# Attention over long keys: both softmax reductions across partitions on GpSimd's all-reduce, with the other small steps moved to ScalarE and VectorE

## The chip, the cores and the metric

The kernel runs on one NeuronCore of one Trainium2 chip. The metric is the time of one execution on the device, in microseconds (us). Of each kernel there is also one execution taken by the hardware profiler; its span runs from the first instruction to the last. In the profile PE is TensorE (PEld its weight loads), DVE is VectorE, ACT is ScalarE, POOL is GpSimd and SP is SyncE, which here only issues DMAs. L12 means line 12 of the kernel's file.

## What is computed

```python
    B, H, Sq, Skv, Dh = 16, 32, 4, 4096, 128      # q, k, v: bf16 normal numbers times 0.05
...
def reference(q, k, v):
    scale = q.shape[-1] ** -0.5
    scores = jnp.einsum('bhqd,bhkd->bhqk', q, k) * scale
    attn = _softmax(scores, axis=-1)
    return jnp.einsum('bhqk,bhkd->bhqd', attn, v)
```

There are 16 x 32 = 512 heads. Each has only 4 query rows, but 4,096 rows of K and as many of V, 1 MB each. So each head reads 2 MB from HBM for 4 rows of output of 128 numbers, and the whole problem reads 1,074 MB.

## The kernel before

The work is done head by head. K and V of two heads (a pair, 2 MB) come with one DMA each into rings of `NBK` and `NBV` buffers (three each). In a buffer, partition p holds 32 consecutive rows of a head (32 chunks of 128 columns), so a chunk is a 128x128 block whose rows are keys.

One step per head, with the code's names:

- `T(h)` on PE transposes the 32 chunks of K against `ident` into the four PSUM tiles `ktp`, eight chunks to a tile. DVE copies three of the four tiles and ACT the fourth (`evac`) into `kT`.
- `QK(h)` on PE multiplies each chunk of `kT` with the four query columns in `qT`. It uses 48 moving columns per chunk (`NPAD`), of which only the first four are wanted; the others are overwritten by the next chunk. The result is 128 columns of scores (32 chunks x 4 queries) in the tile `szo`, keys on the partitions.
- `stageA(h)` on DVE takes the maximum over the chunks for each partition and query into `m1` (128x4). POOL then takes the maximum over the 128 partitions (`partition_all_reduce` into `Mb`, L182), and multiplies by -scale (`negm`, L187).
- `exps(h)` on ACT makes four exponentials, one per query, of 128x32 scores with the bias `negm`, into `eT` (bf16).
- `AV(h)` on PE first multiplies `eT` with a matrix of ones (`ones_bf`, four matmuls of 32 columns, L338), which sums over partitions and leaves the sums per chunk in `szo`. Then it accumulates the 32 chunks of V times `eT` in another part of `szo` (L343).
- `stageB(h)` on DVE adds up the sums over the chunks (`Z4`, L251), takes the reciprocal (`rZ`) and multiplies the output with it into `stage`. After 32 heads, PE transposes the collected 128x128 block, DVE copies it to `ob`, and POOL writes it out by a DMA (16 times).

No scheduler orders this. Each engine runs its own list in program order and waits on semaphores that count finished steps. PE's list is, for step i: `T(i+1)`, `QK(i)`, `AV(i-2)` (`LAG` is 2). DVE's is: three evacuations of head i+1, `stageA(i)`, `stageB(i-2)`. ACT's is: the evacuation of head i+1, `exps(i)`. POOL's is: the all-reduce of head i, then its scaling. SP issues K of pair 0 (its two heads apart), then q by a DMA transpose straight into `qT`, and then in turn K of pair g+1 and V of pair g. A K load waits until the transposes of the pair that used its buffer are done (`s_T`), a V load until the AV of the pair that used its buffer is done (`s_oready`).

Two ties matter for following the steps. `T(h)` may fill the fourth `ktp` tile only when ACT has evacuated the head before, and ACT's evacuation of head i+2 comes after `exps(i)` in ACT's list. The four `szo` tiles are used in turn, so `QK(h)` waits until `stageB(h-4)` is done (`s_fin`).

Of the kernel before, what the change touches and what calls it, by code (L numbers as in the profile page):

```python
# [12 lines left out]
def bass_standalone__softmax_full_bidir__sampling_kernel(  # L13
# [17 lines left out]
    CQ = NCH * NQ  # L31
    CPB = 1024 // P
    assert NCH % CPB == 0
    NU = NCH // CPB
    NPAD = 48
    ZBN = 32
    assert CQ % ZBN == 0
    assert (NCH - 1) * NQ + NPAD <= 2 * CQ and 2 * CQ + NPAD <= 384
    scale = float(D) ** -0.5

    NBK = 3
    NBV = 3
    RT = 3
    R = 4
# [10 lines left out]
    with ExitStack() as es:  # L55
# [5 lines left out]
        vN = sb("vN", [P, NBV, 2, NCH * D], BF16)  # L61
        kT = sb("kT", [P, RT, NCH * P], BF16)
        qT = sb("qT", [P, NHD * NQ + NPAD], BF16)
        eT = sb("eT", [P, R, CQ + NPAD], BF16)
        m1 = sb("m1", [P, R, NQ], FP32)
        Mb = sb("Mb", [P, R, NQ], FP32)
        negm = sb("negm", [P, R, NQ], FP32)
        Z4 = sb("Z4", [P, R, NQ], FP32)
        rZ = sb("rZ", [P, R, NQ], FP32)
        ones_bf = sb("ones_bf", [P, P], BF16)  # L70
        ident = sb("ident", [P, P], BF16)
# [6 lines left out]
        s_q = sem("s_q")  # L78
        s_k0 = sem("s_k0first")
        s_k = [sem(f"s_k{i}") for i in range(NBK)]  # L80
        s_v = [sem(f"s_v{i}") for i in range(NBV)]
# [21 lines left out]

        def zb_slot(r):
            return szo[r][:, CQ:2 * CQ]

        def oT_slot(r):
            return szo[r][:, 2 * CQ:2 * CQ + NQ]

        def oT_acc(r):  # L110
            return szo[r][:, 2 * CQ:2 * CQ + NPAD]

# [15 lines left out]
        @block.sync  # L128
        def _(sp):
            def dma_k(g):  # L130
                slot = g % NBK
                if g == 0:
                    for j, sm in ((0, s_k0), (1, s_k[0])):
                        sp.dma_start(  # L134
                            kN[:, 0, j, :],
                            k_h[j].rearrange("(p c) d -> p (c d)", p=P),
                        ).then_inc(sm, 16)
                    return
                if g >= NBK:
                    sp.wait_ge(s_T, NU * (2 * (g - NBK) + 1) + NU)  # L140
                sp.dma_start(
                    kN[:, slot, :, :],
                    k_h[2 * g:2 * g + 2].rearrange("h (p c) d -> p h (c d)", p=P),
                ).then_inc(s_k[slot], 16)

            def dma_v(g):
                slot = g % NBV
                if g >= NBV:
                    sp.wait_ge(s_oready, 2 * (g - NBV) + 2)
                sp.dma_start(  # L150
                    vN[:, slot, :, :],
                    v_h[2 * g:2 * g + 2].rearrange("h (p c) d -> p h (c d)", p=P),
                ).then_inc(s_v[slot], 16)

            dma_k(0)
            sp.dma_start(qT[:, 0:NHD * NQ], q_rows, transpose=True).then_inc(s_q, 16)
            for g in range(NPAIR):
                if g + 1 < NPAIR:
                    dma_k(g + 1)
                dma_v(g)  # L160

        @block.gpsimd
        def _(pool):
# [12 lines left out]

            for hd in range(NHD):
                r = hd % R
                pool.wait_ge(s_m1, hd + 1)
                if hd >= R:  # L180
                    pool.wait_ge(s_e, hd - R + 1)
                pool.partition_all_reduce(  # L182
                    Mb[:, r, :], m1[:, r, :], P, bass.bass_isa.ReduceOp.max
                ).then_inc(s_pl, 1)
                plc += 1
                pool.wait_ge(s_pl, plc)
                pool.tensor_scalar(negm[:, r, :], Mb[:, r, :], -scale, None, op0=ALU.mult).then_inc(s_negm, 1)  # L187
                if done_grp < NGRP and hd == GH * (done_grp + 1) + 10:
                    dma_out(done_grp)
                    done_grp += 1  # L190
# [6 lines left out]
        def _(act):  # L197
# [4 lines left out]
            def exps(hd):  # L202
                r = hd % R
                act.wait_ge(s_negm, hd + 1)
                if hd >= R:
                    act.wait_ge(s_oready, hd - R + 1)
                e_view = eT[:, r, 0:CQ].rearrange("p (c q) -> p q c", q=NQ)
                s_view = sT_slot(hd % NSZ).rearrange("p (c q) -> p q c", q=NQ)
                ins = None
                for qq in range(NQ):  # L210
                    ins = act.activation(  # L211
                        e_view[:, qq, :], s_view[:, qq, :], ACTF.Exp,
                        bias=negm[:, r, qq:qq + 1], scale=scale,
                    )
                ins.then_inc(s_e, 1)
# [10 lines left out]
        def _(dve):  # L226
            dve.memset(ones_bf[:, :], 1.0).then_inc(s_setd, 1)
            dve.memset(qT[:, NHD * NQ:NHD * NQ + NPAD], 0.0).then_inc(s_setd, 1)
# [7 lines left out]
            def stageA(hd):  # L236
# [6 lines left out]
                ).then_inc(s_m1, 1)  # L243

            def stageB(h2):
                r = h2 % R
                z = h2 % NSZ
                gi = h2 // GH
                col = (h2 % GH) * NQ
                dve.wait_ge(s_oready, h2 + 1)  # L250
                dve.tensor_reduce(  # L251
                    Z4[:, r, :], zb_slot(z).rearrange("p (c q) -> p q c", q=NQ), AX.X, ALU.add
                ).then_inc(s_dv, 1)
                dvc[0] += 1
                dve.wait_ge(s_dv, dvc[0])
                dve.reciprocal(rZ[:, r, :], Z4[:, r, :]).then_inc(s_dv, 1)  # L256
                dvc[0] += 1
                dve.wait_ge(s_dv, dvc[0])
                dve.tensor_tensor(  # L259
                    stage[:, gi, col:col + NQ], oT_slot(z), rZ[:, r, :], ALU.mult  # L260
# [4 lines left out]
            def copy_out(gi):  # L265
                dve.wait_ge(s_tp, gi + 1)
                dve.tensor_copy(ob[:, gi, :], tp_slot((tp_step(gi) + 1) % NSZ)).then_inc(s_ob, 1)  # L267

            for u in DVE_UNITS:
                evac(0, u)  # L270
            for i in range(NHD + LAG):
# [3 lines left out]
                if i < NHD:  # L275
                    stageA(i)
                h2 = i - LAG
                if h2 >= 0:
# [5 lines left out]
        def _(pe):  # L284
            pe.wait_ge(s_q, 16)
            pe.wait_ge(s_setd, 3)
            pe.wait_ge(s_setp, 1)
            pending_ob = []

            def T(h):  # L290
# [3 lines left out]
                for u in range(NU):  # L294
                    if u == 0:
                        if h == 0:
                            pe.wait_ge(s_k0, 16)
                        else:
                            pe.wait_ge(s_k[slot], 16 * (g // NBK + 1))
# [30 lines left out]
            def AV(h2):  # L330
# [4 lines left out]
                pe.wait_ge(s_e, h2 + 1)  # L335
                pe.wait_ge(s_v[slot], 16 * (g // NBV + 1))
                for zc in range(CQ // ZBN):
                    pe.matmul(zb_slot(z)[:, zc * ZBN:(zc + 1) * ZBN], lhsT=ones_bf[:, :],  # L338
                              rhs=eT[:, r, zc * ZBN:(zc + 1) * ZBN], start=True, stop=True)
                vview = vN[:, slot, j, :].rearrange("p (c d) -> p c d", d=D)  # L340
# [56 lines left out]
```

## Time and profile before

| what | value |
|---|---|
| time, median of 4 runs | 8304.77 us (8300.1 to 8309.34) |
| profiled execution, its own time | 8303.16 us |
| its span | 8301.4 us |
| PE, DVE, ACT, POOL busy | 2775.2, 1443.1, 885.1, 343.0 us |
| bytes moved by DMA | 1082.20 MB, mean 130 GB/s |
| granted TensorE clock, mean | 0.637 of full speed |

The profile is to be read like this. A row of a group names the line, the engine, the operation and the tiles (result<-operands), then the count, the busy time of all in us, the mean time of one in ns, and the idle time of the engine just before them with what ended it. A line of the waits names the instruction that waited and the one that released it, then the total in us, the number of times and the longest. "issue" as a releaser means that the profile shows nothing that the engine waited for. In the timeline the columns are start and duration in us, and in square brackets the idle time before. PEclk is the clock that the chip granted TensorE, as a share of full speed. In a table of stretches the columns are the stretch, its length, the busy time of PE, PEld, DVE, ACT and POOL with the number of instructions, PEclk, the busy share of the 16 DMA engines, and GB/s. What POOL's records say of custom instructions such as the all-reduce is rough.

### The profile page before, as it was taken

How to read it: one execution, taken by the hardware profiler on the slowest of the kernel's cores; microseconds unless marked ns; L12 is line 12 of the kernel's file. 1: busy time of each engine (PE TensorE's matmuls, PEld its weight loads, DVE VectorE, ACT ScalarE, POOL GpSimd, SP SyncE). 2: the span in 40 equal slices, each digit the busy share in tenths (PEclk: the TensorE clock that was granted, in tenths of full speed). 3: DMA queues.
4: the chain of work that ended last, by engine and by line, in shares of the span. 5: the costliest groups of instructions: out<-in, count | busy, mean ns of one | idle time of the engine just before them, and what ended most of it. 6: DMA issues, size and time to landing. Idle time of an engine off the chain costs nothing.

```text
span 8301.4 us, 115323 instructions
## 1 busy us (share of the span) xinstructions
PE 2775.2 (33%) x51216; PEld 2687.1 (32%) x51216; DVE 1443.1 (17%) x3603; ACT 885.1 (11%) x2561; POOL 343.0 (4%) x1046
## 2 busy tenths in 40 slices
PE   3333333333333333333333333333333333333332
PEld 3333333333333333333333333333333333333332
DVE  1111111111111111111111111111111111111111
ACT  1111111110111111111111111101111111111111
POOL 0000000000000000000000000000000000000000
PEclk6666666666666666666666666666666666666666
DMA  4333333333333333333333333333333333333331
GB/s 185 123 131 132 132 133 127 128 132 132 133 130 128 129 132 132 131 128 128 132 132 132 132 125 131 132 132 132 124 131 132 132 132 128 128 131 132 132 132 72
DMA packets 142366, 1082.20 MB, mean 130 GB/s; under 512 B 10544, under 2 KB 10544, under 8 KB 10800
## 3 DMA queue, kind: packets, MB, share of 16 engines
q1 hardware_dynamic: 141360, 1074.30, 35.0%
q8 instruction: 406, 6.65, 0.3%
q14 instruction: 88, 0.72, 0.0%
q0 software_dynamic: 512, 0.53, 0.0%
HBM read 1073.74 MB, written 0.52 MB: 129 GB/s over the span
## 4 chain that ended last, share of the span: by engine, by line
issue 69%; PE 14%; ACT 10%; POOL 4%; DVE 2%; POOLq 0%; DMA 0%; SPq 0%; ACTq 0%
PE szo L324 8%; PE ktp L308 6%; ACT kT L200 5%; ACT eT L211 4%; POOL Mb L182 2%; DVE m L241 2%; POOL negm L187 2%; POOLq L187 0%; DMA qT<-in_q_dram 0%; PE szo L343 0%; SPq L134 0%; POOL out_dram L175 0%; PE szo L338 0%; DVE Z L251 0%; PE szo L355 0%
## 5 line engine op out<-in xcount | busy, mean ns | idle before, releaser
L308 PE MATMUL ktp<-ident,kN 128*128 128x128 bf16 x16384 | 1518.5, 266 | 5489.1 <-ACT kT L200 5478.9
L308 PEld LDWEIGHTS ktp<-ident,kN 128*128 128x128 bf16 x16384 | 1312.2, 123 | 5576.5 <-ACT kT L200 5566.3
L211 ACT ACTIVATE eT<-szo,negm 128x32 bf16<-128x32 f32 x2048 | 444.3, 333 | 7396.1 <-POOL negm L187 7396.1
L241 DVE TENSOR_REDUCE m<-szo 128x4 f32<-128x128 f32 x512 | 149.4, 292 | 6182.1 <-PE szo L324 6182.1
L234 DVE COPY kT<-ktp 128x1024 bf16<-128x1024 bf16 x1536 | 985.9, 684 | 76.7 <-PE ktp L308 66.6
L324 PE MATMUL szo<-qT,kT 128*128 128x48 bf16 x16384 | 760.1, 216 | 10.0 <-issue 10.0
L324 PEld LDWEIGHTS szo<-qT,kT 128*128 128x128 bf16 x16384 | 744.5, 120 | 10.1 <-issue 10.1
L343 PE MATMUL szo<-eT,vN 128*128 128x48 bf16 x16384 | 714.7, 211 | 0.0
L343 PEld LDWEIGHTS szo<-eT,vN 128*128 128x128 bf16 x16384 | 661.8, 115 | 0.0
L200 ACT COPY kT<-ktp 128x1024 bf16<-128x1024 bf16 x512 | 527.1, 1029 | 12.6 <-PE ktp L308 12.6
L187 POOL TENSOR_SCALAR negm<-Mb 128x4 f32<-128x4 f32 x512 | 131.9, 258 | 4839.1 <-issue 4839.1
L182 POOL PARTITION_ALL_REDUCE Mb<-m x512 | 198.4, 388 | 3110.2 <-issue 3095.1
L251 DVE TENSOR_REDUCE Z<-szo 128x4 f32<-128x128 f32 x512 | 149.3, 292 | 559.2 <-PE szo L343 559.2
L338 PE MATMUL szo<-eT,ones_bf 128*128 128x32 bf16 x2048 | 144.3, 191 | 22.0 <-ACT eT L211 22.0
L338 PEld LDWEIGHTS szo<-eT,ones_bf 128*128 128x128 bf16 x2048 | 108.1, 111 | 22.2 <-ACT eT L211 22.2
L256 DVE RECIPROCAL rZ<-Z 128x4 f32<-128x4 f32 x512 | 91.3, 178 | 17.4
L259 DVE TENSOR_TENSOR stage<-szo,rZ 128x4 bf16<-128x4 f32 x512 | 82.6, 161 | 17.7
L175 POOL DMA_DIRECT2D out_dram<-ob x16 | 12.0, 750 | 5.1 <-DVE ob L267 4.2
L355 PE MATMUL szo<-ident,stage 128*128 128x128 bf16 x16 | 4.1, 253 | 0.8 <-DVE stage L259 0.8
L267 DVE COPY ob<-szo 128x128 bf16<-128x128 bf16 x16 | 3.4, 214 | 0.4 <-PE szo L355 0.4
L355 PEld LDWEIGHTS szo<-ident,stage 128*128 128x128 bf16 x16 | 1.7, 107 | 0.9 <-DVE stage L259 0.9
L200 ACT ACT_TABLE_LOAD x1 | 1.3, 1283 | 0.7 <-PEq L382 0.7
(9 smaller groups left out, 1.3 us busy)
## 6 DMA issues: line engine op xcount, KB each, us to landing
vN<-in_v_dram SPq DMA_DIRECT2D x256, 2048.0 KB, 7.5
kN<-in_k_dram SPq DMA_DIRECT2D x255, 2048.0 KB, 8.6
kN<-in_k_dram SPq DMA_DIRECT2D x2, 1024.0 KB, 6.0
out_dram<-ob POOLq DMA_DIRECT2D x16, 32.0 KB, 1.9
qT<-in_q_dram SPq DMA_TRANSPOSE x1, 8.5
```

Of the source, the lines that this page charges most:

```text
L182: pool.partition_all_reduce(Mb[:, r, :], m1[:, r, :], P, bass.bass_isa.ReduceOp.max).then_inc(s_pl, 1)
L187: pool.tensor_scalar(negm[:, r, :], Mb[:, r, :], -scale, None, op0=ALU.mult).then_inc(s_negm, 1)
L200: act.copy(kT[:, h % RT, u * CPB * P:(u + 1) * CPB * P], ktp[u][:, :]).then_inc(s_eva, 1)
L211: ins = act.activation(e_view[:, qq, :], s_view[:, qq, :], ACTF.Exp, bias=negm[:, r, qq:qq + 1], scale=scale,)
L234: dve.tensor_copy(kT[:, h % RT, u * CPB * P:(u + 1) * CPB * P], ktp[u][:, :]).then_inc(s_evd, 1)
L241: dve.tensor_reduce(m1[:, r, :], sT_slot(hd % NSZ).rearrange("p (c q) -> p q c", q=NQ), AX.X, ALU.max).then_inc(s_m1, 1)
L251: dve.tensor_reduce(Z4[:, r, :], zb_slot(z).rearrange("p (c q) -> p q c", q=NQ), AX.X, ALU.add).then_inc(s_dv, 1)
L256: dve.reciprocal(rZ[:, r, :], Z4[:, r, :]).then_inc(s_dv, 1)
L308: ins = pe.transpose(ktp[u][:, cc * P:(cc + 1) * P], kview[:, c, :], ident[:, :])
L324: ins = pe.matmul(szo[z][:, c * NQ:c * NQ + NPAD], lhsT=ktv[:, c, :], rhs=qT[:, hd * NQ:hd * NQ + NPAD], start=True, stop=True,)
L338: pe.matmul(zb_slot(z)[:, zc * ZBN:(zc + 1) * ZBN], lhsT=ones_bf[:, :], rhs=eT[:, r, zc * ZBN:(zc + 1) * ZBN], start=True, stop=True)
L343: ins = pe.matmul(oT_acc(z), lhsT=vview[:, c, :], rhs=eT[:, r, c * NQ:c * NQ + NPAD], start=(c == 0), stop=(c == NCH - 1),)
```

## The change

- POOL no longer scales the maximum. It now does two all-reduces per head: the maximum of head i, and then the sum of head i-1 (`sum_ar`). Both are `partition_all_reduce`.
- The scaling to `negm` moves to ACT, ahead of the exponentials of the same head.
- The sum of a head's exponentials over the chunks moves to DVE (`rowsum`, on `eT`), which makes `rsum` (128x4) for POOL's sum. The matmuls with ones, the tile `ones_bf` and DVE's reduction over their result are gone. `szo` is laid out anew.
- `stageB` takes the reciprocal of POOL's sum, and waits for the output of AV only ahead of the product.
- q comes by a plain DMA into `qN`; PE transposes it in 16 blocks and DVE copies the blocks to `qT` with 16 copies.
- K has four buffers instead of three, and K of pair g+2 (no longer g+1) is issued after V of pair g. The last pair of K and V comes as two DMAs each, one per head, with a semaphore of its own for the first.

```diff
...
     NGRP = NHD // GH
     CQ = NCH * NQ
     CPB = 1024 // P
     assert NCH % CPB == 0
     NU = NCH // CPB
     NPAD = 48
-    ZBN = 32
-    assert CQ % ZBN == 0
-    assert (NCH - 1) * NQ + NPAD <= 2 * CQ and 2 * CQ + NPAD <= 384
+    OTC = 192
+    assert (NCH - 1) * NQ + NPAD <= OTC and OTC + NPAD <= 384
+    NQC = (NHD * NQ) // P
+    assert (NHD * NQ) % P == 0 and NQC <= 2 * CPB_
     scale = float(D) ** -0.5
 
-    NBK = 3
+    NBK = 4
     NBV = 3
     RT = 3
     R = 4
...
         kN = sb("kN", [P, NBK, 2, NCH * D], BF16)
         vN = sb("vN", [P, NBV, 2, NCH * D], BF16)
         kT = sb("kT", [P, RT, NCH * P], BF16)
+        qN = sb("qN", [P, NQC * D], BF16)
         qT = sb("qT", [P, NHD * NQ + NPAD], BF16)
         eT = sb("eT", [P, R, CQ + NPAD], BF16)
...
+        rsum = sb("rsum", [P, R, NQ], FP32)
...
-        ones_bf = sb("ones_bf", [P, P], BF16)
...
         def sT_slot(r):
             return szo[r][:, 0:CQ]
 
-        def zb_slot(r):
-            return szo[r][:, CQ:2 * CQ]
-
         def oT_slot(r):
-            return szo[r][:, 2 * CQ:2 * CQ + NQ]
+            return szo[r][:, OTC:OTC + NQ]
 
         def oT_acc(r):
-            return szo[r][:, 2 * CQ:2 * CQ + NPAD]
+            return szo[r][:, OTC:OTC + NPAD]
 
         def tp_slot(r):
             return szo[r][:, 384:448].bitcast(BF16)
...
         def _(sp):
             def dma_k(g):
                 slot = g % NBK
-                if g == 0:
-                    for j, sm in ((0, s_k0), (1, s_k[0])):
+                if g >= NBK:
+                    sp.wait_ge(s_T, NU * (2 * (g - NBK) + 1) + NU)
+                if g == 0 or g == NPAIR - 1:
+                    first = s_k0 if g == 0 else s_klast
+                    for j, sm in ((0, first), (1, s_k[slot])):
                         sp.dma_start(
-                            kN[:, 0, j, :],
-                            k_h[j].rearrange("(p c) d -> p (c d)", p=P),
+                            kN[:, slot, j, :],
+                            k_h[2 * g + j].rearrange("(p c) d -> p (c d)", p=P),
                         ).then_inc(sm, 16)
                     return
-                if g >= NBK:
-                    sp.wait_ge(s_T, NU * (2 * (g - NBK) + 1) + NU)
                 sp.dma_start(
                     kN[:, slot, :, :],
                     k_h[2 * g:2 * g + 2].rearrange("h (p c) d -> p h (c d)", p=P),
...
                 slot = g % NBV
                 if g >= NBV:
                     sp.wait_ge(s_oready, 2 * (g - NBV) + 2)
+                if g == NPAIR - 1 and g > 0:
+                    for j, sm in ((0, s_vlast), (1, s_v[slot])):
+                        sp.dma_start(
+                            vN[:, slot, j, :],
+                            v_h[2 * g + j].rearrange("(p c) d -> p (c d)", p=P),
+                        ).then_inc(sm, 16)
+                    return
                 sp.dma_start(
                     vN[:, slot, :, :],
                     v_h[2 * g:2 * g + 2].rearrange("h (p c) d -> p h (c d)", p=P),
                 ).then_inc(s_v[slot], 16)
 
             dma_k(0)
-            sp.dma_start(qT[:, 0:NHD * NQ], q_rows, transpose=True).then_inc(s_q, 16)
+            sp.dma_start(qN[:, :], q_rows.rearrange("(p c) d -> p (c d)", p=P)).then_inc(s_q, 16)
+            if NPAIR > 1:
+                dma_k(1)
             for g in range(NPAIR):
-                if g + 1 < NPAIR:
-                    dma_k(g + 1)
                 dma_v(g)
+                if g + 2 < NPAIR:
+                    dma_k(g + 2)
 
         @block.gpsimd
         def _(pool):
...
                 pool.wait_ge(s_ob, gi + 1)
                 pool.dma_start(out_rows[gi * P:(gi + 1) * P, :], ob[:, gi, :]).then_inc(s_out, 16)
 
-            for hd in range(NHD):
-                r = hd % R
-                pool.wait_ge(s_m1, hd + 1)
-                if hd >= R:
-                    pool.wait_ge(s_e, hd - R + 1)
+            def sum_ar(h2):
+                r = h2 % R
+                pool.wait_ge(s_rs, h2 + 1)
                 pool.partition_all_reduce(
-                    Mb[:, r, :], m1[:, r, :], P, bass.bass_isa.ReduceOp.max
-                ).then_inc(s_pl, 1)
-                plc += 1
-                pool.wait_ge(s_pl, plc)
-                pool.tensor_scalar(negm[:, r, :], Mb[:, r, :], -scale, None, op0=ALU.mult).then_inc(s_negm, 1)
+                    Z4[:, r, :], rsum[:, r, :], P, bass.bass_isa.ReduceOp.add
+                ).then_inc(s_zall, 1)
+
+            for hd in range(NHD + 1):
+                if hd < NHD:
+                    r = hd % R
+                    pool.wait_ge(s_m1, hd + 1)
+                    if hd >= R:
+                        pool.wait_ge(s_e, hd - R + 1)
+                    pool.partition_all_reduce(
+                        Mb[:, r, :], m1[:, r, :], P, bass.bass_isa.ReduceOp.max
+                    ).then_inc(s_pl, 1)
+                    plc += 1
+                if hd >= 1:
+                    sum_ar(hd - 1)
                 if done_grp < NGRP and hd == GH * (done_grp + 1) + 10:
                     dma_out(done_grp)
                     done_grp += 1
...
 
             def exps(hd):
                 r = hd % R
+                act.wait_ge(s_pl, hd + 2)
+                act.mul(negm[:, r, :], Mb[:, r, :], -scale).then_inc(s_negm, 1)
                 act.wait_ge(s_negm, hd + 1)
                 if hd >= R:
                     act.wait_ge(s_oready, hd - R + 1)
...
 
         @block.vector
         def _(dve):
-            dve.memset(ones_bf[:, :], 1.0).then_inc(s_setd, 1)
             dve.memset(qT[:, NHD * NQ:NHD * NQ + NPAD], 0.0).then_inc(s_setd, 1)
             dve.memset(eT[:, :, CQ:CQ + NPAD], 0.0).then_inc(s_setd, 1)
             dvc = [0]
...
                     m1[:, r, :], sT_slot(hd % NSZ).rearrange("p (c q) -> p q c", q=NQ), AX.X, ALU.max
                 ).then_inc(s_m1, 1)
 
+            def rowsum(h1):
+                r = h1 % R
+                dve.wait_ge(s_e, h1 + 1)
+                if h1 >= R:
+                    dve.wait_ge(s_zall, h1 - R + 1)
+                dve.tensor_reduce(
+                    rsum[:, r, :], eT[:, r, 0:CQ].rearrange("p (c q) -> p q c", q=NQ), AX.X, ALU.add
+                ).then_inc(s_rs, 1)
+
             def stageB(h2):
                 r = h2 % R
                 z = h2 % NSZ
                 gi = h2 // GH
                 col = (h2 % GH) * NQ
-                dve.wait_ge(s_oready, h2 + 1)
-                dve.tensor_reduce(
-                    Z4[:, r, :], zb_slot(z).rearrange("p (c q) -> p q c", q=NQ), AX.X, ALU.add
-                ).then_inc(s_dv, 1)
-                dvc[0] += 1
-                dve.wait_ge(s_dv, dvc[0])
+                dve.wait_ge(s_zall, h2 + 1)
                 dve.reciprocal(rZ[:, r, :], Z4[:, r, :]).then_inc(s_dv, 1)
                 dvc[0] += 1
                 dve.wait_ge(s_dv, dvc[0])
+                dve.wait_ge(s_oready, h2 + 1)
                 dve.tensor_tensor(
                     stage[:, gi, col:col + NQ], oT_slot(z), rZ[:, r, :], ALU.mult
                 ).then_inc(s_fin, 1)
...
                 dve.wait_ge(s_tp, gi + 1)
                 dve.tensor_copy(ob[:, gi, :], tp_slot((tp_step(gi) + 1) % NSZ)).then_inc(s_ob, 1)
 
+            dve.wait_ge(s_qT, 1)
+            qTv = qT[:, 0:NHD * NQ].rearrange("d (p c) -> d c p", c=NQC)
+            for c in range(NQC):
+                dve.tensor_copy(qTv[:, c, :], ktp[c // CPB][:, (c % CPB) * P:(c % CPB + 1) * P]).then_inc(s_setd, 1)
             for u in DVE_UNITS:
                 evac(0, u)
             for i in range(NHD + LAG):
...
                         evac(i + 1, u)
                 if i < NHD:
                     stageA(i)
+                if 1 <= i <= NHD:
+                    rowsum(i - 1)
                 h2 = i - LAG
                 if h2 >= 0:
                     stageB(h2)
...
         @block.tensor
         def _(pe):
             pe.wait_ge(s_q, 16)
-            pe.wait_ge(s_setd, 3)
             pe.wait_ge(s_setp, 1)
+            qNv = qN[:, :].rearrange("p (c d) -> p c d", d=D)
+            ins = None
+            for c in range(NQC):
+                ins = pe.transpose(ktp[c // CPB][:, (c % CPB) * P:(c % CPB + 1) * P], qNv[:, c, :], ident[:, :])
+            ins.then_inc(s_qT, 1)
+            pe.wait_ge(s_setd, 2 + NQC)
             pending_ob = []
 
             def T(h):
...
                     if u == 0:
                         if h == 0:
                             pe.wait_ge(s_k0, 16)
+                        elif g == NPAIR - 1 and j == 0:
+                            pe.wait_ge(s_klast, 16)
                         else:
                             pe.wait_ge(s_k[slot], 16 * (g // NBK + 1))
                     if h >= 1:
...
                 r = h2 % R
                 z = h2 % NSZ
                 pe.wait_ge(s_e, h2 + 1)
-                pe.wait_ge(s_v[slot], 16 * (g // NBV + 1))
-                for zc in range(CQ // ZBN):
-                    pe.matmul(zb_slot(z)[:, zc * ZBN:(zc + 1) * ZBN], lhsT=ones_bf[:, :],
-                              rhs=eT[:, r, zc * ZBN:(zc + 1) * ZBN], start=True, stop=True)
+                if g == NPAIR - 1 and j == 0 and g > 0:
+                    pe.wait_ge(s_vlast, 16)
+                else:
+                    pe.wait_ge(s_v[slot], 16 * (g // NBV + 1))
                 vview = vN[:, slot, j, :].rearrange("p (c d) -> p c d", d=D)
                 ins = None
                 for c in range(NCH):
```

## The prediction

> **What bounds the kernel now.** I read the busy shares first, then the waits, then the rows of the two POOL instructions, then the timeline of one head and of the end.
>
> ```profile
> PE 2775.2 (33%) x51216; PEld 2687.1 (32%) x51216; DVE 1443.1 (17%) x3603; ACT 885.1 (11%) x2561; POOL 343.0 (4%) x1046
> ...
> q1 hardware_dynamic: 141360, 1074.30, 35.0%
> ...
> issue 69%; PE 14%; ACT 10%; POOL 4%; DVE 2%; POOLq 0%; DMA 0%; SPq 0%; ACTq 0%
> ```
>
> No engine is busy over 33%, the 16 DMA engines 35%, and the chain of waits is 69% "issue": an engine that stands although nothing recorded holds it. The waits say which engine:
>
> ```profile
> ACT eT L211 <- POOL negm L187: 7396.1, 512, 18.4
> DVE m L241 <- PE szo L324: 6182.1, 512, 15.8
> ...
> PE ktp L308 <- ACT kT L200: 5478.9, 509, 14.2
> POOL negm L187 <- issue: 4839.1, 512, 12.7
> POOL Mb L182 <- issue: 3095.1, 511, 10.0
> ```
>
> PE waits for ACT, ACT waits for POOL's negm, and only POOL waits for nothing. POOL alone adds up to the span: 198.4 us of all-reduces, 131.9 of scalings, and 4839.1 + 3095.1 us of "issue" before them are 8264.5 of 8301.4 us. Per head that is 0.39 + 9.45 + 0.26 + 6.05 = 16.1 us. What sits in the gaps shows in the records of the two lines and in the timeline of one head:
>
> ```profile
> L182 POOLq MODIFY_POOL_CONFIG  x1024: 8/11/37, 1.7 to 8280.5; - x171
> ...
> L187 POOLq MODIFY_POOL_CONFIG  x1024: 82/83/83, 17.2 to 8286.4; - x171
> ```
> ```profile
> 4019.93 0.26 POOL L187 TENSOR_SCALAR negm<-Mb 128x4 f32<-128x4 f32 x1 [10.49 <-issue]
> 4020.22 0.87 ACT L211 ACTIVATE eT<-szo,negm 128x32 bf16<-128x32 f32 x4 [15.48 <-POOL negm L187]
> ...
> 4026.06 0.39 POOL L182 PARTITION_ALL_REDUCE Mb<-m  x1 [5.87 <-issue]
> ```
>
> Before each all-reduce and each scaling POOL is reconfigured, and then stands for 6 to 10 us. The maximum of a head is ready well before (DVE's reduction at 4024.36 us ended at 4024.65, the all-reduce began at 4026.06), so data is not what it waits for. The alternation all-reduce, scaling, all-reduce is what costs 15.5 us of 16.2 per head.
>
> **The change part by part.** *The alternation goes.* The built program of the changed kernel has one reconfiguration ahead of the first all-reduce and then 1,024 all-reduces, two per head, with no other computation on POOL; its 16 output DMAs stay. So 512 x (9.45 + 6.05) = 7936 us of gaps leave POOL, and 132 us of scalings. What is unknown is the true length of an all-reduce, since its record ends at 0.39 us while the scaling that needs its result starts 9.45 us later. Two heads at the end, when no loads run any more, bound it:
>
> ```profile
> 8272.15 0.39 POOL L182 PARTITION_ALL_REDUCE Mb<-m  x1 [5.91 <-issue]
> 8279.94 0.26 POOL L187 TENSOR_SCALAR negm<-Mb 128x4 f32<-128x4 f32 x1 [7.40 <-issue]
> ...
> 8286.03 0.39 POOL L182 PARTITION_ALL_REDUCE Mb<-m  x1 [5.83 <-issue]
> 8293.27 0.26 POOL L187 TENSOR_SCALAR negm<-Mb 128x4 f32<-128x4 f32 x1 [6.85 <-issue]
> ```
>
> From below it is its record, 0.39 us (386 to 392 ns in all 512). From above it is 0.39 + 6.85 = 7.2 us, if the second reconfiguration were free. If both cost alike, 6.85 - 5.83 = 1.0 us is left over and it is 1.4 us. Here the Trainium skill says more: its "GPSIMD Engine Reference", section 2.1 (Instruction dispatch), has the first call after a load of new code pay about 6 us that no instruction shows. The 5.83 to 6.05 before the all-reduce agree. But subtracting the page's 6 us from the mean 9.45 would leave 3.5 us to the all-reduce, so 3.9 us each, 7.8 per head, and about 4,000 us in all. The same gap, however, is 6.85 where no transfers run and 12.69 at the start where they are densest, and work inside POOL has no reason to do that; loading of code has. I take 0.4 to 1.4 us, nearest to the record: POOL then needs 0.9 to 2.9 us per head (two, and about 0.05 of hand-over each).
>
> *What is late next.* Per head, at the full clock of the first 20 us:
>
> PE: a head's 32 transposes take 1.79 us and its QK 0.91 (timeline at 16.18 and 17.92 us). AV is seen only at half clock, 1.33 us against 1.46 for QK there, so about 0.85 to 0.9. The four matmuls with ones (0.21) go. Sum 3.6 us.
>
> DVE: three evacuations 1.89 us in a row, the maximum 0.29, the new row sum (nearest row: the maximum, of equal shape, 0.29; bounds 0.15 to 0.6), reciprocal 0.18, product 0.16. The old sum over szo (0.29) leaves. Sum 2.8 us.
>
> ACT: evacuation 1.03, four exponentials 0.87, the new negm on 128x4 (nearest: one exponential, 0.22 to 0.33) 0.25. Sum 2.2 us.
>
> DMA: 2.1 MB per head. The stretches of the first 44 us show what the DMA engines give when several transfers queue and PE, DVE and ACT work beside them:
>
> ```profile
> 12.00:44.00 32.00, 14.23 (x270) 13.89 (x267) 10.53 (x21) 3.75 (x7) 1.04 (x3) 0.74 1.01 421
> 10.00:45.00 35.00, 16.00 (x284) 15.66 (x284) 11.22 (x21) 3.75 (x7) 1.04 (x3) 0.75 1.00 412
> ```
>
> (The last two columns are the share of the DMA engines and GB/s.) 2.097 MB at 421 GB/s is 4.98 us per head, above all three engines. So DMA becomes the bound. A page speaks against that rate: the Trainium skill, "DMA: Bandwidth & Descriptors", Specifications, gives a core about 358 GB/s of its HBM. By it the 1,082 MB take 3,022 us, by the row 2,570. The row stands; a page figure below what 32 us of this trace moved is no bound for a core that runs alone.
>
> *The new waits.* The chain through a head is maximum 0.29, all-reduce 0.39 to 1.4, negm 0.25, exponentials 0.87, evacuation 1.03, the last eight transposes 0.45, QK 0.91: 4.2 to 5.2 us, and some 1.2 of hand-overs. ACT's evacuation of head i+2 stands behind the exponentials of head i, so this chain spans two heads and asks 2.7 to 3.2 us per head, under DMA's 4.98. On ACT the exponentials and the next evacuation now queue behind negm (0.25, inside the chain). On DVE the row sum of head i-1 waits for exponentials that ended about a head earlier; the product and the next evacuations are queued behind it, and the transposes behind those. On POOL the maximum of head i+1 is queued behind the sum of head i-1, whose row sum is ready about a head earlier; the output DMA stands there too, behind DVE's copy of a group that ended many heads before. Until now that DMA came right after a scaling, now it comes between all-reduces; if that alone cost two loads of code, 16 x 15.5 = 248 us of POOL is the bound from above, none from below, and four queued transfers (20 us of DMA) cover one such stop. I take nothing. The reciprocal waits for a sum asked for a head earlier. At 5 us per head each has 1.5 us or more to spare: I cost them at nothing, and at up to 0.3 us per head if DMA were not the cover.
>
> *Buffers, order and ends.* Four K pairs instead of three and K issued two pairs ahead let SP hold about four 2 MB transfers in the queue, as in the stretch above, so I take the queue as never dry. Each issue costs SP 0.37 to 0.57 us. The q load is a plain 0.5 MB copy, 1.2 us of DMA; the DMA transpose that held SP from 1.66 to 8.15 us is gone. PE's 16 transposes (0.9 us) and DVE's 16 copies (nearest row L267, 0.21 us; 3.4, perhaps twice that with their scattered writes) delay the first head from 10.2 to about 13 us, while SP has loads queued for 30 us: nothing on DMA's path. Splitting the last pairs saves under one 1 MB transfer, 2.5 us, at the end.
>
> *Sum.* Bytes 1,082 MB at 421 GB/s: 2,570 us; ramp of the first 4 us (53 and 262 GB/s) 2.5; from the last byte to the end about 8 (now 6.9 from the last AV's start to the end). That is 2,580; at 412 GB/s it is 2,637. I lean a quarter of the way to the lower rate: span 2,595. The profiled execution took 8303.16 us around a span of 8301.4, so 1.8 is added: 2,597 us. That execution lies 1.6 us under the median of 8304.77, which changes nothing here.
>
> **The rivals.** *PE at half clock.* PEclk read 0.50 in all idle stretches, and with DMA as the bound PE rests 1.4 us of 5. At half clock the transposes take 3.1 us (eight in 0.77), QK 1.46, AV 1.33: 5.9 per head, about 3,020 us. Against it: bursts of 5 us as at 4024 us brought the clock to 1.00, and a PE at half speed would have no rest. It can hold part of the time, 2,680 to 3,020.
>
> *POOL stays the bound because an all-reduce is longer than its record.* It decides from 2.5 us each (2 x 2.5 = 4.98). At 3.9 us 4,000 us, at 7.2 us 7,500. For it: records of POOL are rough. Against it: the quiet gaps above.
>
> *The code is loaded anyway*, for maximum and sum in turn: 2 x (0.39 + 6.05) = 12.9 us per head, 6,600 us. Against it: the program holds one reconfiguration.
>
> *Slower: the 9.45 us after an all-reduce are its own.* If POOL takes that time after every all-reduce, whatever follows, two per head cost 2 x (0.39 + 9.45) = 19.7 us, 10,080 us. It turns slower from 8.1 us each. Against it are the 6.85 us of the quiet end, which alone are below that point.
>
> **How the numbers follow.** DMA-bound 0.75 (2,530 at 430 GB/s to 2,680 at 405), PE clock 0.12, POOL bound by longer all-reduces 0.08, code loaded anyway 0.03, slower 0.02. The range runs from 2,530 over the DMA case and most of the clock case to 2,920; above it lie the last of the clock case and the POOL cases. A measurement of this kernel can tell about 0.2% from no change; faster than that 0.97, within it 0.01, slower 0.02.
>
> **What would show it.** Right: no "issue" wait of microseconds on POOL; the DMA share near ten tenths with 410 to 425 GB/s in every slice but the first and last; PE waiting for transfers of kN or vN; PEclk near 1.0; all-reduce starts not tied to each other. Wrong: PE busy throughout at PEclk 0.5 (clock), POOL's two all-reduces back to back with equal gaps and all others waiting for Mb or Z (POOL), or a DMA share of ten tenths below 400 GB/s (rate mis-sized).

## The result, and the profile after

| | median | runs |
|---|---|---|
| kernel before | 8303.16 us | 13 (8292.11 to 8310.43) |
| changed kernel | 2629.86 us | 8 (2627.91 to 2631.26) |

The ratio is 0.3167, with a 95% interval of 0.3164 to 0.317. The forecast was 2,597 us in a range of 2,530 to 2,920; the measured time is 33 us (1.3%) above the forecast. The profiled execution took 2627.91 us around a span of 2626.1.

The page of the changed kernel, where the page before had 33% as the busiest engine and the DMA engines at 35%:

```profile
PE 2011.2 (77%) x49184; PEld 1971.2 (75%) x49184; DVE 1371.2 (52%) x3618; ACT 1069.0 (41%) x3073; POOL 409.4 (16%) x1046
...
PEclk9999988988999999888888898988989999988889
DMA  9999999999999999999999999999999999999998
GB/s 403 419 419 419 419 419 417 415 413 415 415 414 415 413 414 413 411 413 415 411 412 418 418 410 415 413 413 414 416 410 415 414 416 410 413 413 416 411 412 333
...
q1 hardware_dynamic: 139456, 1074.30, 99.1%
q8 instruction: 390, 6.39, 1.0%
...
DMA 78%; PE 19%; issue 2%; DVE 0%; POOL 0%; ACT 0%; SPq 0%; POOLq 0%; DVEq 0%
```

Read it from below: the chain that ended last was 69% "issue" and is now 78% DMA. The DMA row is nine tenths or more in 39 of 40 slices, and the rate is near 415 GB/s where it was near 130. The granted clock is 0.903 of full speed in the mean, up from 0.637.

The waits (who waited, for whom, total us, times, longest):

```profile
POOL Mb L205 <- DVE m L265: 2198.3, 512, 18.5
...
PE ktp L350 <- DMA kN<-in_k_dram: 465.1, 234, 3.8
...
ACT negm L228 <- POOL Mb L205: 373.7, 512, 2.6
```

The two "issue" waits of POOL, 7,934 us together, are gone: POOL now stands because DVE has no maximum for it yet. The records of reconfigurations, 1,024 each for the all-reduce and for the scaling before, have gone down to two at the start:

```profile
L205 POOLq MODIFY_POOL_CONFIG  x2: 1/1/1, 11.9 to 12.0; - x2
```

ACT waits 0.7 us per head for POOL, where it waited 14.4. The longest wait of PE in total is for K from HBM. The timeline of POOL and its neighbours in one head shows the two all-reduces following each other, and the scaling on ACT starting 0.04 us after the first one's record:

```profile
1503.33 0.37 POOL L205 PARTITION_ALL_REDUCE Mb<-m  x1 [3.27 <-DVE m L265]
...
1503.61 0.51 POOL L195 PARTITION_ALL_REDUCE Z<-rsum  x1
...
1503.74 0.20 ACT L228 ACTIVATE negm<-Mb 128x4 f32<-128x4 f32 x1 [1.18 <-POOL Mb L205]
```

### The profile page after: what moved, and what is told of

Its sections match the earlier page's. It is cut to its first block, busy times and chain, and to the rows that moved or that the text cites. A ratio compares the mean times of both kernels' runs of the same rounds, so it can differ in the third digit from the quotient of the medians.

```text
span 2626.1 us, 110762 instructions
## 1 busy us (share of the span) xinstructions
PE 2011.2 (77%) x49184; PEld 1971.2 (75%) x49184; DVE 1371.2 (52%) x3618; ACT 1069.0 (41%) x3073; POOL 409.4 (16%) x1046
## 4 chain that ended last, share of the span: by engine, by line
DMA 78%; PE 19%; issue 2%; DVE 0%; POOL 0%; ACT 0%; SPq 0%; POOLq 0%; DVEq 0%
DMA kN<-in_k_dram 78%; PE ktp L350 12%; PE szo L366 4%; PE szo L385 4%; DVE qT L301 0%; PE ktp L325 0%; DVE kT L258 0%; ACT kT L223 0%; POOL out_dram L190 0%; PE szo L397 0%; SPq L163 0%; POOL ident L181 0%; DVE ob L296 0%; POOL ident L179 0%; DVE stage L288 0%
## 5 line engine op out<-in xcount | busy, mean ns | idle before, releaser
L350 PE MATMUL ktp<-ident,kN 128*128 128x128 bf16 x16384 | 1161.5, 237 | 489.8 <-DMA kN<-in_k_dram 465.1
L350 PEld LDWEIGHTS ktp<-ident,kN 128*128 128x128 bf16 x16384 | 1068.5, 107 | 518.6 <-DMA kN<-in_k_dram 489.8
L223 ACT COPY kT<-ktp 128x1024 bf16<-128x1024 bf16 x512 | 518.3, 1012 | 1158.3 <-PE ktp L350 1158.3
L385 PE MATMUL szo<-eT,vN 128*128 128x48 bf16 x16384 | 520.1, 185 | 71.3 <-issue 71.0
L366 PE MATMUL szo<-qT,kT 128*128 128x48 bf16 x16384 | 536.5, 188 | 37.4 <-issue 32.8
L366 PEld LDWEIGHTS szo<-qT,kT 128*128 128x128 bf16 x16384 | 507.4, 99 | 39.1 <-issue 35.3
L385 PEld LDWEIGHTS szo<-eT,vN 128*128 128x128 bf16 x16384 | 469.6, 97 | 80.8 <-issue 80.5
L195 POOL PARTITION_ALL_REDUCE Z<-rsum x512 | 258.8, 505 | 2.6 <-DVE rsum L274 2.4
L228 ACT ACTIVATE negm<-Mb 128x4 f32<-128x4 f32 x512 | 105.3, 206 | 373.7 <-POOL Mb L205 373.7
L274 DVE TENSOR_REDUCE rsum<-eT 128x4 f32<-128x128 bf16 x512 | 141.4, 276 | 0.6 <-issue 0.2
```

The lines of the kernel that those rows point to most:

```text
L195: pool.partition_all_reduce(Z4[:, r, :], rsum[:, r, :], P, bass.bass_isa.ReduceOp.add).then_inc(s_zall, 1)
L223: act.copy(kT[:, h % RT, u * CPB * P:(u + 1) * CPB * P], ktp[u][:, :]).then_inc(s_eva, 1)
L228: act.mul(negm[:, r, :], Mb[:, r, :], -scale).then_inc(s_negm, 1)
L274: dve.tensor_reduce(rsum[:, r, :], eT[:, r, 0:CQ].rearrange("p (c q) -> p q c", q=NQ), AX.X, ALU.add).then_inc(s_rs, 1)
L350: ins = pe.transpose(ktp[u][:, cc * P:(cc + 1) * P], kview[:, c, :], ident[:, :])
L366: ins = pe.matmul(szo[z][:, c * NQ:c * NQ + NPAD], lhsT=ktv[:, c, :], rhs=qT[:, hd * NQ:hd * NQ + NPAD], start=True, stop=True,)
```

## The experiments

The theory is that the alternation of two kinds of POOL instruction was the whole cost, and that the stream of K and V is what is left. The rivals: the deeper K ring and the new loads did it; the all-reduce itself is long; the engines and not DMA are the new bound. A last group asks why the changed kernel is 33 us slower than forecast.

**One part alone: the scaling on ACT.** The kernel before, with only this edit:

```diff
 # POOL, after partition_all_reduce(...).then_inc(s_pl, 1)
-                pool.wait_ge(s_pl, plc)
-                pool.tensor_scalar(negm[:, r, :], Mb[:, r, :], -scale, None, op0=ALU.mult).then_inc(s_negm, 1)
 # ACT, at the head of exps(hd)
+                act.wait_ge(s_pl, hd + 2)
+                act.mul(negm[:, r, :], Mb[:, r, :], -scale).then_inc(s_negm, 1)
```

> The kernel before with one part of the change alone: the scaling to negm moves from POOL to ACT. POOL keeps one all-reduce per head; the sums stay with the matmuls with ones, K keeps three buffers, q its DMA transpose. If the alternation of code on POOL was the whole bound, this alone reaches the DMA bound: 2,600 to 2,700 us, at 410 GB/s or more in the middle. If the second all-reduce, the K ring or the loads issued two pairs ahead are needed as well, it stays well above: PE's four matmuls with ones add 0.2 us per head, which DMA covers, and a queue with only two or three transfers in it would show a DMA share under nine tenths and 2,750 us or more.

Measured: 2635.19 us, ratio 0.3172 (0.3167 to 0.3177). Its runs (2634.18 to 2636.18) all lie above those of the changed kernel (2627.91 to 2631.26), by 5 us in the median; the intervals of the two ratios overlap, so whether these 5 us are the rest of the change or the difference between two sets of runs stays open. This edit of two lines out and two lines in brings 5,676 us, and the second all-reduce, the row sums, the K ring and the q load together bring 5 us at most. What they take from PE (matmuls with ones) DMA was covering.

**The same part undone.** The changed kernel, with the scaling put back on POOL behind the all-reduce of the maximum, and taken from ACT.

> The changed kernel with the scaling put back on POOL, between the two all-reduces: POOL's order per head is maximum, scaling, sum, so it is reconfigured twice per head as before. If the reconfiguration is the cost, POOL again needs 0.4 + 9.5 + 0.26 + 6.0 + 0.3 us per head, about 16.5, and the time is 8,300 to 8,700 us, slower than the kernel before or equal to it. If instead what helped was the rest of the change (K ring, q load, sums), it stays far below 8,000 us.

Measured: 8399.6 us, ratio 1.0109 (1.0089 to 1.0129): all the rest of the change in place, and 1.1% slower than the kernel before (two runs). The timeline of POOL shows where the stops come back:

```profile
4000.63 0.26 POOL L210 TENSOR_SCALAR negm<-Mb 128x4 f32<-128x4 f32 x1 [10.89 <-issue]
4006.86 0.44 POOL L195 PARTITION_ALL_REDUCE Z<-rsum  x1 [5.98 <-issue]
4007.23 0.45 POOL L205 PARTITION_ALL_REDUCE Mb<-m  x1
4014.41 0.26 POOL L210 TENSOR_SCALAR negm<-Mb 128x4 f32<-128x4 f32 x1 [6.73 <-issue]
```

Two all-reduces in a row have no gap between them. A gap stands at each change of kind: about 6 us ahead of the first all-reduce, 6.7 and 10.9 us ahead of these two scalings (the longest of all is 13.5). The means are 3108.1/511 = 6.1 us and 4695.6/512 = 9.2 us.

**The true length of an all-reduce.** The changed kernel, with 32 more per head behind the sum:

```diff
+                for x in range(32):
+                    ins = pool.partition_all_reduce(
+                        junk[:, x, :], rsum[:, r, :], P, bass.bass_isa.ReduceOp.add
+                    )
```

> The changed kernel with 32 more all-reduces per head on POOL, whose results nobody uses: 34 per head. This measures what an all-reduce really takes when they follow each other. At the recorded 0.37 to 0.51 us each, 12.6 to 17 us per head, 6,500 to 8,900 us. If they overlap at the 0.28 us between the starts of two in the trace after, 9.5 us per head, 4,900 us. If an all-reduce were 1.4 us or more, as the estimate from the quiet gaps allowed, 48 us per head and 24,000 us.

Measured: 7170.55 us (two runs). POOL is now the bound; its timeline (start, duration):

```profile
4004.21 13.25 POOL L203 PARTITION_ALL_REDUCE junk<-rsum  x32
4017.36 0.45 POOL L214 PARTITION_ALL_REDUCE Mb<-m  x1
```

From one start to the next they take 13.15 / 32 = 0.41 us each, and the span agrees: 7168.9 / 512 heads / 34 = 0.41. So the all-reduce is about as long as its record, and the 9.45 us that stood after it in the kernel before was not its own work. The changed kernel shows the same from the other side: ACT takes the result of an all-reduce 0.04 us after its record ends. This removes three things: the estimate of up to 1.4 us, the 3.9 us that came from subtracting a fixed load, and the rival in which the change is slower.

**Loads alone.** The DMAs of the changed kernel in the same order and rings, each load waiting only for the one before it in its buffer; no computation, the output filled from q.

> The DMAs of the changed kernel alone: all of K, V and q are loaded in the same order into the same rings, a load waits only for the one before it in its buffer, nothing is computed, and the output is filled from q. If the changed kernel is bound by DMA alone, this takes its time less the end and the ramps: 2,590 to 2,625 us, at 412 to 416 GB/s. If the engines' traffic in SBUF or the instruction fetches (1.1% of the DMA engines' time) slow the transfers, it reaches 421 GB/s as at the start, 2,560 us or less.

Measured: 2563.06 us. The expectation for "bound by DMA alone" (2,590 us or more) missed; the time is 3 us from the other one, in which the engines' traffic or the instruction fetches slow the transfers. The loads could run 67 us (2.5%) faster than in the changed kernel. Its rate is 422 GB/s in every slice but the first and last:

```profile
GB/s 405 422 422 422 422 422 422 422 422 422 422 422 422 422 422 422 422 422 422 422 422 422 422 422 422 422 422 422 422 422 422 422 422 422 422 422 422 422 422 347
```

**The engines alone.** The changed kernel, loading K only for the first four pairs and V for the first three; all later pairs work on these buffers again.

> The changed kernel without its stream: K is loaded for the first four pairs and V for the first three, and all later pairs work on these buffers again. This shows what the engines need once DMA is out of the way. By the prediction's sum PE at full clock is next, 3.6 us per head: 1,850 to 1,950 us with PEclk 1.00 nearly throughout. If the engines' own chain of waits (DVE, ACT, POOL) or the clock were near the bound, it would be 2,400 us or more.

Measured: 1774.74 us, 3.47 us per head, PE busy 98% at clock 0.999. PE is next, as forecast, but the time lies 75 us under the range expected here (1,850), since PE needs less than the 3.6 us per head of the sum. There are 855 us between it and the changed kernel. So neither PE's work nor the chain through POOL and ACT sets the pace.

**A fourth V buffer.** The changed kernel with `NBV = 4`.

> The changed kernel with four V buffers instead of three. In the trace after, the GB/s fall to 320 to 340 from 2,600 us on and SP issues the last V pair only at 2,603 us, because it waits for AV of three pairs before; the missing bytes of that stretch are worth some 7 us. With one more buffer the last V is issued a pair earlier: 2,619 to 2,625 us, 0.2 to 0.4% less. If the last transfers are slow for another reason, or the queue elsewhere is never short, no difference to the changed kernel.

Measured: 2627.67 us (2627.14 to 2628.11), 2 us under the changed kernel, within the spread of the two sets of runs. The last V pair was indeed issued ten microseconds earlier (2593.42 instead of 2603.00 us), and the end came no sooner. The stretches before the end say why (the last two columns are the share of the DMA engines and GB/s):

```profile
2600.00:2604.00 4.00, 4.00 (x90) 4.00 (x88) 2.64 (x6) 1.01 (x1) 0.20 (x1) 0.72 0.52 219
2604.00:2608.00 4.00, 3.32 (x94) 3.21 (x89) 2.61 (x7) 2.46 (x8) 1.36 (x4) 1.00 0.51 207
2608.00:2612.00 4.00, 3.48 (x100) 3.49 (x100) 2.48 (x7) 1.71 (x5) 0.05 (x1) 1.00 0.51 213
2612.00:2616.00 4.00, 2.75 (x71) 2.58 (x67) 2.28 (x6) 1.49 (x6) 0.73 (x2) 1.00 0.51 207
```

For 16 us half of the DMA engines' time is idle at half of the rate, though everything has been issued. The records of the single transfers say which idle time this is: from 2,600 to 2,616 us eight packets are in flight nearly all the time, where 16 were before. So eight of the 16 engines are done and eight still have a backlog, and the kernel ends when these end. In the loads-only kernel there is no such stretch: there the packets in flight fall from 16 to one within 2 us, at 2,548 to 2,550.

**What makes them lag: PE's instructions.** The loads-only kernel with a PE stream beside it that waits for no load and touches none of the data:

```diff
+            for h in range(NHD):
+                for c in range(NCH):
+                    pe.transpose(ktp[c // CPB][:, (c % CPB) * P:(c % CPB + 1) * P], ident[:, :], ident[:, :])
+                for c in range(2 * NCH):
+                    pe.matmul(szo[h % NSZ][:, 0:NPAD], lhsT=ident[:, :], rhs=ident[:, 0:NPAD], start=True, stop=True)
```

> The loads-only kernel with a stream of PE instructions beside it that waits for nothing and reads only the identity: per head 32 transposes and 64 matmuls of 48 columns, as many as the changed kernel has, and no work on DVE and ACT. It adds PE's instruction fetch to the DMA engines and hardly any other traffic. If the fetches are what takes the changed kernel's rate from 422 to 414 GB/s, the loads take 20 to 30 us longer than alone (2,580 to 2,592 us), with a lower rate only while PE runs (some 1,800 us), and the last microseconds run at a part of the DMA engines, since the fetches burden some of them more. If the traffic of the engines in SBUF is the cause, 2,565 us and 422 GB/s, as alone.

Measured: 2630.4 us in one run, the time of the changed kernel. The stretches (here PE, PEld, POOL, then clock, share and GB/s):

```profile
100.00:500.00 400.00, 317.40 (x8339) 311.57 (x8336) 0.00 (x0) 0.96 1.01 419
500.00:1000.00 500.00, 404.73 (x10459) 396.91 (x10457) 0.00 (x0) 0.95 1.01 414
1000.00:1500.00 500.00, 395.03 (x10422) 387.75 (x10420) 0.00 (x0) 0.97 1.01 412
...
2000.00:2300.00 300.00, 240.57 (x6307) 236.25 (x6303) 0.00 (x0) 0.96 1.01 412
2300.00:2500.00 200.00, 44.62 (x1185) 43.62 (x1184) 0.00 (x0) 0.63 1.01 420
2500.00:2560.00 60.00, 0.00 (x0) 0.00 (x0) 0.00 (x0) 0.50 1.01 422
...
2600.00:2610.00 10.00, 0.00 (x0) 0.00 (x0) 0.00 (x0) 0.50 0.58 244
2610.00:2620.00 10.00, 0.00 (x0) 0.00 (x0) 0.00 (x0) 0.50 0.41 171
```

While PE runs, the rate is 419 in the first 500 us and 412 from 1,000 us on, though PE does the same in both; once PE has ended (at 2,356 us) it is 422. At the very end, more than 200 us after PE's last instruction, eight packets are again in flight instead of 16 for some 15 us. The direction and the low rate were expected, but the time of 2,580 to 2,592 us missed: the loss (67 us) is more than twice the 26 us that the 1.0% share of the instruction queue makes if it is spread evenly (0.010 x 2,629). The loads' own packets take longer too: 99.2% of 2,628.6 us on 16 engines here against 100.8% of 2,561.4 alone, 26 us more; why is not shown. And PE suffers too. It waits for nothing in this kernel, yet its waits are

```profile
PE szo L149 <- issue: 385.4, 247, 2.1
...
PE ktp L147 <- issue: 87.2, 105, 1.2
```

which is 473 us in 352 stops. The instruction queue moved 384 packets, 6.29 MB, so one packet is 16 KB, and PE stops about once per packet. In the kernel that works without its stream the same kind of stop is there once, for 2.2 us, so it takes the full DMA engines to make them.

**The whole computation beside free loads.** The loads-only kernel and the changed kernel's computation on one pair's K and V in buffers of its own. It loads 4.2 MB more (10 us at 421 GB/s) and does not fill the output at the end.

> The loads-only kernel with the whole computation beside it, which works on one pair's K and V in buffers of its own and waits for no other load: the instruction fetch and the traffic of all engines in SBUF and PSUM, but no wait between loads and computation. If fetches alone are the cause, as long as the run with the PE stream, within 5 us. If the engines' traffic adds to it, longer by 10 us or more, 2,600 us, with the lower rate up to about 1,780 us, where the computation ends. If the changed kernel's last 20 us come from the waits between loads and computation, this one ends at 2,590 us or less.

Measured: 2632.03 us in one run. The loads of this one end with the kernel, at 2,630 us, those of the run before at 2,619.6, where its output begins; the difference of 10.6 us is the 4.2 MB. So DVE, ACT and POOL with their traffic add nothing that one run of each can tell to what PE's instructions cost, and taking away the waits between loads and computation gains nothing. The computation did not end at 1,780 us as expected, but at 2,490: PE stood 520 us in 337 "issue" stops.

**Fewer instructions, as much work.** PE gets 16 matmuls of 512 columns per head, 8,192 in all where the narrow stream had 49,152.

> The loads-only kernel with a PE stream of a sixth as many instructions, but of wide matmuls: 16 of 512 columns per head, no transposes. PE is as busy as in the run with the narrow stream, or busier, and reads as much from SBUF, but its instructions are a sixth. If it is the fetching of instructions that slows the loads (67 us for the narrow stream), a sixth of it remains: 2,574 us. If it is PE's own traffic in SBUF, or the power that it draws, 2,620 us or more.

Measured: 2572.16 us in one run, against 2,574 expected from a sixth of the instructions. PE was busy 1761.1 us, near the 1882.0 of the narrow stream, and the rate stayed at 421 GB/s. (PE's row counts 8,029 of the 8,192 matmuls; the others have no record.)

```profile
PE 1761.1 (69%) x8029; PEld 801.8 (31%) x8192; POOL 1.2 (0%) x7
...
q8 instruction: 64, 1.05, 0.2%
```

The loss goes with the bytes of instructions (9 us for 1.05 MB of them, 67 us for 6.29) and not with the busy time of PE's matmuls. One rival is left: the text above says that PE reads as much from SBUF, but its weight loads have gone down to a sixth too (8,192 for 49,152), so this run alone can't tell fetches from weight loads. Against weight loads speak the stops of PE, about one per packet, and the rate of the narrow stream, which was 419 in one stretch and 412 in a later one with as many weight loads per us. A narrow stream that fetches little, or wide matmuls with many weight loads, was not run.

**An attempt to even out the lag.** The changed kernel with six V pair loads cut into 16 DMAs of 8 partitions each.

> The changed kernel with six of its 256 V pair loads (every 43rd) each cut into 16 DMAs of 8 partitions, so that such a load is not spread over 128 rows at once. The reason: in the runs with a PE stream, the last transfers ran at half of the DMA engines for 20 us and more, so some of the engines lag, by the instruction fetches that they carry. If DMAs of 8 rows use only a part of the engines, and those are the ones that do not lag, the load is evened out and the time falls by up to 35 us, to about 2,595 us. If they fall on the lagging ones, 2,660 to 2,690 us. If they spread over all, or the lag is of another origin, 2,630 us or a few us more for SP's 16 issues.

Measured: 2757.81 us (2752.5 to 2759.14), worse than all three expectations: 128 us for six loads, 21 us each. The rate around one of them falls to 307, 219 and 198 GB/s in three stretches of 10 us while the DMA engines read as fully busy. Cut this way a transfer is far slower, but which engines it used does not show, so this says nothing on which of them lag.

## Why the prediction was right, and where 33 us came from

*What bounds before*: right. POOL's row sum to the span, and the one edit and its undoing move the whole 5,670 us. The word "reconfigured" is shown as far as a trace can: per head the stops stand at changes of kind and nowhere else, and the records of reconfigurations go from 2,048 to two. What happens inside a stop no trace shows.

*Length of an all-reduce*: 0.41 us, at the low end of the 0.4 to 1.4 taken. Of the two readings of the 9.45 us gap, the one from the quiet end of the trace was right, and subtracting the 6 us of the Trainium skill ("GPSIMD Engine Reference", section 2.1) from it would have been wrong: the stop ahead of the scaling is itself 6.7 us or more in the traces read.

*Engines next*: PE 3.47 us per head against 3.6 (and it keeps PEclk at 0.999 when it does not wait). DVE's busy time is 1371.2 / 512 = 2.7 against 2.8, ACT's 2.1 against 2.2. The new waits cost nothing that shows: DVE waited 0.6 us in all ahead of its row sums, and POOL 2.4 us ahead of the sums. One sign did not come: "all-reduce starts not tied to each other". The sum follows the maximum at once in 511 of 512 heads, and yet POOL is not the bound, as its wait for DVE's maximum shows.

*DMA bound at 421 GB/s, not 358*: right as to what bounds, and the measured rate stays well above the 358 of the Trainium skill ("DMA: Bandwidth & Descriptors", Specifications), as far as a core that runs alone goes. The term that was mis-sized is this one. "I lean a quarter of the way to the lower rate" put the bytes at 2,584 us; from 500 us on the changed kernel ran at 413 to 414. The trace of before held 421 GB/s in a stretch of 32 us, about the rate of the loads alone (422). So short a stretch could not show the loss: the changed kernel itself moves 419 GB/s from 12 to 44 us and 418 up to 500 us, and falls to 414 only after that. What the sum left out is that the instructions, 6.4 MB for PE, cost more than their bytes: 67 us, shown with PE's stream, and 9 us with a sixth of its instructions. In the terms of the forecast: K, V and q alone, 1,074.3 MB at 422 GB/s, are 2,546 us, so its 2,584 left 38 us for the instructions' bytes and the lean; 67 are 29 more, of the 33 us missed. The other 4 are not broken down. That the forecast came within 1.3% owes something to the lean, which had no working behind it.

*Split of the last pairs, K ring*: forecast at next to nothing, and nothing measurable. *Start*: forecast a first head at 13 us, measured 22.5. Two terms were too small: DVE's 16 copies of q took 8.69 us (3.4 to 6.8 forecast), and POOL made the identity only at 11.42 us. DMA covered both, as argued: 397 to 434 GB/s in every 4 us from 4 us on.

*PE clock*: 0.90, between the two cases, with no effect as DMA is the bound. The forecast read 0.50 "in all idle stretches"; in the first 10 us of the same trace, where PE had not begun, the records say 1.00.

*Still open*: which DMA engines carry the fetches, and whether the loss can be evened out. The eight engines of the end fit with eight carrying all fetches: 384 packets of 1.07 us are 51 us on each of eight, for the 67 lost, and the 64 of the wide matmuls 8.6 us, for the 9 lost. But no record names the engine of a packet, so that is argued, not shown. No version here beat the changed kernel by more than the spread of its runs.

## What to carry to other kernels

When no engine is busy and the chain of waits is "issue", look for the engine whose own row plus its "issue" waits add up to the span, and then at what changes between its neighbouring instructions: here one small scaling on POOL between all-reduces cost 15.5 us per head, and two lines moved it to ACT. Before rating the parts of a large change, run the one that the profile points at alone. When a stream of loads becomes the bound, check its rate against the loads alone; the rest of the gap may be instruction fetch. Here a PE stream of fewer and wider instructions cost the loads less.

## What the runs showed of the hardware that was not expected

- The code that POOL holds seems to outlast the execution. In every kernel whose last POOL computation is an all-reduce, making the identity at the start waits for 10.5 to 12.0 us (10.49 in the changed kernel); in the kernel before, whose last one is a scaling, it waits 0.50, and in the loads with wide matmuls, which have no all-reduce, 0.23. That the execution before is the reason is inferred:

```profile
11.42 0.28 POOL L181 TENSOR_SCALAR_AFFINE_SELECT ident<-ident 128x128 bf16<-128x128 bf16 x1 [10.49 <-issue]
```

- PE's instructions come in packets of 16 KB, and the loads beside them slow down (422 to 412 GB/s). With the DMA engines full, PE stops for 1 to 2 us about once per packet (473 us in 352 stops in the run with the PE stream), and in the changed kernel for 119.6 us in 113 stops.
- The records of all-reduces overlap a little: the second of a pair starts 0.28 us after the first, whose record lasts 0.37.
- The output DMAs of POOL, now among all-reduces, show no stop (0.56 us each), though they land after 5.9 us instead of 1.9 under the full load.
